# Retention mixer on one core: two turns for a chunk, first weights widened in pairs, projection tokens loaded ahead, key weights fetched in halves

## The chip, the cores and the metric

The kernel runs on one core of a Trainium2 chip. The metric is the time of one execution in microseconds on the device. TensorE (PE) does the matrix products; VectorE (DVE), ScalarE (ACT) and GpSimd (POOL) convert, copy and add; SyncE (SP) does nothing but issue DMA transfers, one after the other.

## The reference

Three layers follow each other over 8 batches of 576 positions and 512 channels. The weights come as float64.

```python
# retention: 8 heads of 64
scores = scale * q @ k.T
Dmat   = where(rel >= 0, gamma[h] ** rel, 0)
x      = (scores * Dmat) @ v                    # (8, 576, 512)
# low-rank mix along the sequence (rank 32), then an MLP
h  = x.T @ U @ V
u  = x + h.T
x2 = u + relu(u @ w_ch1) @ w_ch2                # 512 -> 2048 -> 512
# channel mix with the row before
xk = mu_k * x2 + (1 - mu_k) * x2_prev
xr = mu_r * x2 + (1 - mu_r) * x2_prev
k  = relu(xk @ w_k)                             # 512 -> 1024
out = sigmoid(xr @ w_r) * (k * k @ w_v)         # 1024 -> 512
```

## The kernel before

All products run as three passes over float32 numbers cut in a high and a low part (`split`: ScalarE casts the high part, `h`; another engine subtracts it, `l`): high by high weight, high by low weight, low by high weight. The float64 weights are brought in as pairs of words and turned into float32 by `widen` (L132 to L146: one ACT and four DVE instructions), then split.

Attention goes over 40 chunks, five to a batch (four of 128 rows and one of 64). `chunk_step` writes a chunk's TensorE work: `ds` (state), `xn` (transpose), `x` (values), `g` (the low-rank sum of the chunk before) and `s` (scores of the chunk after). VectorE masks the scores into `pm`, on which `x` depends. When a batch is through, `gt` is summed and eight mixes `mx` follow, whose results VectorE adds to `xt`; then `xt` is stored as `u` to DRAM (`ub`), in blocks of 512 rows that the nine blocks t of the MLP use. `hidden_tokens(t)` loads a block of u back, casts it (`uh`) and subtracts (`u` then holds the low part).

`hidden` gives, for each of the nine blocks, 16 tiles of 12 matmuls (`h_g_q`), which are fed into the attention, one at a time. `w1`, the first weight, is converted in eight units of 128x1024; a unit's low part is `w1l`. Tiles with an even q need units 0 to 3, tiles with an odd q units 4 to 7. ReLU results `h_o` go to DRAM (`hb`).

The projection (`Project`) has nine blocks of eight steps; a step takes one loaded piece of h (`y_x`), builds sums of blocks (`y_t`, mostly POOL), splits it (`y_kh` on ACT, low part on DVE) and does 42 matmuls for seven products. At a block's end `sums` combines eight PSUM banks on DVE into `y_s`, POOL adds u (`uin`) and the block x2 is stored (`xb`). Keys, gate and values follow, block by block: `load_x2` brings a block of x2 in (`x2in`), `mix_row` makes `m_x` and `zx` on ACT and DVE.

Three things set the order. TensorE's instructions stand in the order in which the code writes them. On the other engines a scheduler orders them by priority: the conversion of weights (`background`) stands behind the rest. SP issues the DMAs in its own order, and one that must wait holds all behind it. Weights of later phases go to DRAM and come back through `fetches`, when `limit` lets them, and all big tiles share one pool of 20 buffers (`RAWS`).

```python
for _ in chunk_step(i) ...:      # four turns to a chunk
    mixes(2 if i < JOIN else 1)
    pump(1 if i < 4 else 3 if i < JOIN else 2)
    drive(1)
```

`mixes(n)` writes so many mixes, `pump(n)` so many steps of weight conversion, `drive(n)` so many steps of the token loads in `ahead`. From chunk JOIN on, 16/5 hidden tiles go with each chunk.

## Time and profile before

| | |
|---|---|
| median of two runs | 1569.79 us (1569.6 to 1569.98) |
| profiled execution | 1573.2 us |
| its span | 1571.4 us |
| PE busy | 1469.6 us (94%) |
| DVE, ACT, POOL busy | 863.1, 561.8, 542.0 us |
| mean granted TensorE clock | 0.966 |

TensorE is busy nearly all the time, so a reader looks for the few places where it is not. In the page's slices it falls below full in the first three (up to 118 us), at 629 to 668 us, and from about 1021 us on. The granted clock is lowest in the same slices.

### The profile page before, as it was taken

The page shows a single profiled execution, that of the slowest core. Times are in us where ns is not written, and L with a number is a line of the kernel's source. Part 1 is how long each engine was busy: PE and PEld are TensorE (multiplying, and loading weights), DVE is VectorE, ACT ScalarE, POOL GpSimd, SP SyncE. Part 2 cuts the span into 40 slices and gives each one's busy share as a digit, 9 for nine tenths or more (in the row PEclk, how much of TensorE's full clock was granted, in tenths as well). Part 3 has the DMA queues.
Part 4 walks back from the last instruction along what each step waited for, and adds up shares of the span by engine and source line. Part 5 has one row for each costly group of instructions (what it writes and reads, how often), then busy time and mean ns, then how long its engine had stood idle before and what let it go on. Part 6 is the DMA issues. An engine that isn't in the chain of part 4 may idle for free. (4 is left out here: it accounts for less than half of the span.)

```text
span 1571.4 us, 24443 instructions
## 1 busy us (share of the span) xinstructions
PE 1469.6 (94%) x10164; PEld 1283.1 (82%) x10164; DVE 863.1 (55%) x1020; ACT 561.8 (36%) x822; POOL 542.0 (34%) x480
## 2 busy tenths in 40 slices
PE   7659999999999999699999999978999998999998
PEld 5547777777777888599999999978888888788887
DVE  4894554455631100278888888657676676443321
ACT  2533544444443222233333333244444445231210
POOL 3142433331210000267788778644334333000000
PEclk8869999999999999799999999989999999999999
DMA  9476897879834832724444444643323223875521
GB/s 322 169 266 215 310 331 287 311 268 344 321 146 165 343 134 105 290 96 147 159 150 162 161 158 151 227 189 133 135 111 131 108 111 131 329 281 206 205 103 54
DMA packets 76302, 312.97 MB, mean 199 GB/s; under 512 B 10080, under 2 KB 18528, under 8 KB 58272
## 3 DMA queue, kind: packets, MB, share of 16 engines
q1 hardware_dynamic: 76192, 311.42, 54.2%
q8 instruction: 80, 1.31, 0.3%
q14 instruction: 30, 0.25, 0.0%
HBM read 188.70 MB, written 122.68 MB: 198 GB/s over the span
## 5 line engine op out<-in xcount | busy, mean ns | idle before, releaser
L303 POOL TENSOR_TENSOR y_t<-y_x 128x256 f32<-128x256 f32 x72 | 81.6, 1133 | 256.1 <-DMA y_x<-hb 246.7
L412 PE MATMUL h<-uh,w1h 128*128 128x512 f32 x576 | 162.5, 404 | 1.8 <-ACT xt L575 1.8
L303 POOL TENSOR_TENSOR y_t<-y_x,y_t 128x256 f32<-128x256 f32 x144 | 160.1, 1112 | 11.3
L436 ACT ACTIVATE h_o<-h 128x512 f32<-128x512 f32 x144 | 84.7, 598 | 220.0 <-PE h L412 219.8
L412 PE MATMUL h<-uh,w1l 128*128 128x512 f32 x576 | 156.1, 393 | 0.9 <-DVE w1l L155 0.9
L412 PE MATMUL h<-u,w1h 128*128 128x512 f32 x576 | 155.2, 391 | 0.0
L412 PEld LDWEIGHTS h<-uh,w1l 128*128 128x128 f32 x576 | 108.9, 189 | 25.5 <-DVE w1l L155 1.3
L412 PEld LDWEIGHTS h<-u,w1h 128*128 128x128 f32 x576 | 108.7, 189 | 23.6
L490 POOL TENSOR_TENSOR qkv<-qkv,qtab 128x512 f32<-128x512 f32 (+1 forms) x35 | 46.7, 1333 | 225.0 <-DMA qkv<-in_qkv 169.5
L412 PEld LDWEIGHTS h<-uh,w1h 128*128 128x128 f32 x576 | 102.7, 189 | 24.3 <-issue 3.7
L303 DVE TENSOR_TENSOR y_t<-y_x 128x256 f32<-128x256 f32 x72 | 62.0, 861 | 89.1 <-DMA y_x<-hb 88.8
L303 POOL TENSOR_TENSOR m_x<-m_x 128x256 f32<-128x256 f32 x72 | 84.6, 1193 | 72.6 <-DVE m_x L900 54.5
L982 DVE TENSOR_TENSOR rin<-v,rin 128x512 f32<-128x512 f32 x36 | 24.8, 690 | 114.4 <-PE v L412 114.3
L516 DVE TENSOR_TENSOR pm<-s,mask 128x512 f32<-128x512 f32 (+1 forms) x80 | 47.6, 629 | 67.4 <-PE s L507 67.4
L412 PE MATMUL v<-vh,wvh 128*128 128x512 f32 x288 | 73.1, 395 | 3.4 <-ACT vh L153 3.4
L153 ACT CAST vh<-v 128x1024 fp32r<-128x1024 f32 x36 | 36.1, 1051 | 105.2 <-PE v L412 63.1
L412 PE MATMUL v<-vh,wvl 128*128 128x512 f32 x288 | 72.7, 396 | 0.0
L412 PE MATMUL v<-v,wvh 128*128 128x512 f32 x288 | 71.2, 389 | 0.0
L360 POOL TENSOR_TENSOR k_o<-k_o 128x512 f32<-128x512 f32 x18 | 23.8, 1324 | 127.0 <-issue 39.1
L412 PEld LDWEIGHTS v<-vh,wvh 128*128 128x128 f32 x288 | 54.2, 190 | 16.4 <-ACT vh L153 5.4
L878 POOL TENSOR_TENSOR uin<-uin,y_s 128x512 f32<-128x512 f32 x36 | 55.5, 1564 | 31.3 <-DVE y_s L377 31.2
L412 PEld LDWEIGHTS v<-vh,wvl 128*128 128x128 f32 x288 | 55.2, 192 | 11.7
(293 smaller groups left out, 4160.3 us busy)
## 6 DMA issues: line engine op xcount, KB each, us to landing
hb<-h_o SPq DMA_DIRECT2D x36, 1024.0 KB, 5.0
y_x<-hb SPq DMA_DIRECT2D x72, 512.0 KB, 4.7
qkv<-in_qkv SPq DMA_DIRECT2D x64, 512.0 KB, 7.5
kb<-k_o SPq DMA_DIRECT2D x18, 1024.0 KB, 3.9
v<-kb SPq DMA_DIRECT2D x18, 1024.0 KB, 6.9
u<-ub SPq DMA_DIRECT2D x9, 1024.0 KB, 9.8
uin<-ub SPq DMA_DIRECT2D x9, 1024.0 KB, 5.0
xb<-uin SPq DMA_DIRECT2D x9, 1024.0 KB, 4.8
```

Source lines behind the costliest of these rows:

```text
L153: nc.scalar.copy(h, x)
L303: engines[n % len(engines)].tensor_tensor(o, i, j, op=ALU.subtract)
L360: nc.gpsimd.tensor_tensor(c[1][1], c[1][1], c[1][0], op=ALU.add)
L412: nc.tensor.matmul(ps, weight.part(lo, k, o), x, start=(i == 0), stop=(i == len(todo) - 1))
L436: nc.scalar.activation(tile_of(outs[g], q), ps, AF.Relu)
L490: eng.tensor_tensor(q, q, qtab[:, c, :, :n], op=ALU.mult)
L516: nc.vector.tensor_tensor(p[:n, g, :, :n], ps[g][:n, :, :n], mask[:n, :, :n].to_broadcast([n, NP, n]), op=ALU.mult,)
L878: nc.gpsimd.tensor_tensor(v[:, i, :, j], v[:, i, :, j], c[i][j], op=ALU.add)
L982: nc.vector.tensor_tensor(r[:, o], ps, r[:, o], op=ALU.mult)
```

## The change

The chunk step yields twice instead of four times; the numbers per turn are doubled. `g` of the chunk before now stands ahead of `s` of the chunk after. Hidden tiles may begin with chunk 7 instead of 11, and before each tile the code makes sure that the four units of w1 that it needs are converted; block 0 takes the eight tiles with even q first, as the last block does. While w1 is converted, two units are pumped in turn, and the low part of w1 is subtracted by GpSimd, not VectorE.

In the projection, `begin` (loads and splits of the first pieces) is written inside the last hidden block, ten tiles from the end, instead of behind the last tile. At a block's end the splits of the next block's second piece and of its third stand in other places: `cut(s + 2)` runs at k = 7 ahead of `sums`, and `uin` is loaded at k = 4 instead of 0. The weights `wk[1]` and `wr` are asked for behind the projection's loop, not ahead of it.

```diff
--- before.py
+++ after.py
@@ -36,7 +36,7 @@
 RAWS = 20
 MORE = 5
-JOIN = 11
+JOIN = 7
 RATE = 16 / 5
@@ -92,20 +92,27 @@
     begun = set()
     ahead = []
+
+    width = [1]
+    turn = [0]
+
+    def step(x):
+        begun.add(id(x))
+        with tc.high_priority(offset=-LOW):
+            next(x)
+
     def pump(n):
         while n and background:
-            for x in background[1:2]:
+            for x in background[width[0]:width[0] + 1]:
                 if id(x) not in begun:
-                    begun.add(id(x))
-                    with tc.high_priority(offset=-LOW):
-                        next(x)
-            begun.add(id(background[0]))
+                    step(x)
+            turn[0] += 1
+            x = background[turn[0] % min(width[0], len(background))]
             try:
-                with tc.high_priority(offset=-LOW):
-                    next(background[0])
+                step(x)
                 n -= 1
             except StopIteration:
-                background.pop(0)
+                background.remove(x)
     def drive(n=None):
         while ahead and (n is None or n > 0):
@@ -149,10 +156,10 @@
         )
         yield
-    def split(h, l, x):
+    def split(h, l, x, eng=nc.vector):
         nc.scalar.copy(h, x)
         yield
-        nc.vector.tensor_tensor(l, x, h.bitcast(F32), op=ALU.subtract)
+        eng.tensor_tensor(l, x, h.bitcast(F32), op=ALU.subtract)
         yield
     def slot(x, i):
@@ -211,7 +218,7 @@
             self.per = 1024 // self.cols or 1
             self.units = self.rows * self.cols // 1024
-            self.parts = None
+            self.parts, self.finished = None, 0
         def keep(self):
             self.parts = [[raw(F32R, f"{self.nm}{lo}{i}") for i in range(self.units // 2)] for lo in "hl"]
@@ -244,7 +251,8 @@
             f, a = x[:, 1024:], x[:, :1024]
             yield from widen(f, a, w)
             if direct:
-                yield from split(self.unit(0, u), self.unit(1, u), f)
+                yield from split(self.unit(0, u), self.unit(1, u), f, nc.gpsimd)
+                self.finished += 1
                 return
             yield from split(a.bitcast(F32R), f.bitcast(F32R), f)
             for lo, y in enumerate((a, f)):
@@ -393,6 +401,7 @@
     tokens = {}
     stored = set()
+    done_tiles = [0]
     def hidden_tokens(t):
         x = raw(F32, f"u{t}")
@@ -424,13 +433,15 @@
             now = [(tile_of(h, k), tile_of(l, k), k) for k in range(KD)]
             asked = False
             tiles = [(g, q) for g in range(4) for q in range(4)]
-            if t == NB - 1:
+            if t in (0, NB - 1):
                 tiles.sort(key=lambda x: x[1] % 2)
             outs, missing = {}, {}
             for g, q in tiles:
                 if g not in outs:
                     outs[g], missing[g] = raw(F32, f"h{t}_{g}_o"), 4
+                while w1.finished < (q % 2 + 1) * w1.rows:
+                    pump(1)
                 ps = bank(f"h{t}_{g}_{q}")
                 plain(ps, q % 2 * 8 + g * 2 + q // 2, w1, now)
                 nc.scalar.activation(tile_of(outs[g], q), ps, AF.Relu)
@@ -651,7 +662,7 @@
         def later(b):
-            todo.extend([lambda: None] * 3)
+            todo.extend([lambda: None] * 2)
             for s in range(2):
                 for k in range(KD):
                     todo.append(lambda k=k, s=s: mix(b, k, s))
@@ -747,11 +758,7 @@
                 state(b, c)
             if i > 0:
                 natural(*seq[i - 1])
-            yield
             values(b, c, qs.pop(i))
-            yield
-            if i + 1 <= LAST:
-                scores(*seq[i + 1])
             yield
             if i > 0:
                 pb, pc = seq[i - 1]
@@ -759,6 +766,8 @@
                 if pc == NC - 1:
                     low_rank_sum(pb)
                     later(pb)
+            if i + 1 <= LAST:
+                scores(*seq[i + 1])
             yield
         def end_step():
@@ -778,33 +787,35 @@
         def later_weights():
             if not asked:
                 asked.append(1)
-                pump(1000)
+                width[0] = 1
                 background.extend(w.prepare() for w in (*w2, *wk[0], *wk[1]))
                 background.extend(wr.prepare(u, False) for u in range(wr.units))
                 background.extend(wv.prepare(u, False) for u in range(wv.units))
         def advance():
-            more = next(along, None)
-            return more is False
+            more = next(along, None) is False
+            done_tiles[0] += more
+            return more
         started = False
         for i in range(LAST + 2):
             if i == W_START:
                 w1.keep()
                 background.extend(w1.prepare(u, True) for u in range(w1.units))
+                width[0] = 2
             for _ in chunk_step(i) if i <= LAST else end_step():
-                mixes(2 if i < JOIN else 1)
+                mixes(4 if i < JOIN else 2)
                 if not started and 0 in stored:
                     ahead.append(hidden_tokens(0))
                     started = True
-                pump(1 if i < 4 else 3 if i < JOIN else 2)
-                drive(1)
+                pump(2 if i < 4 else 6 if w1.finished < w1.units else 4)
+                drive(2)
                 if i < JOIN:
                     continue
-                if i == JOIN:
+                if w1.finished == w1.units:
                     later_weights()
-                due += RATE / 4
+                due += RATE / 2
                 while due >= 1:
                     due -= 1
                     if not advance():
@@ -854,10 +865,12 @@
         def run(self):
             for s, (t, k) in enumerate(self.steps):
                 self.load(s + 2)
-                self.cut(s + 1)
+                if k or not t:
+                    self.cut(s + 1)
                 self.blocks(s + 2)
                 if k == 0:
                     acc = {p: bank(f"y{t}_{i}") for i, p in enumerate(ORDER)}
+                if k == 4:
                     u_in[t] = raw(F32, f"uin{t}")
                     nc.sync.dma_start(u_in[t].rearrange("p (k n) -> p k n", k=KD), u_blk[t])
                 assert w2[k].ready, k
@@ -868,6 +881,7 @@
                 if t == NB - 1:
                     w2[k].free()
                 if k == 7:
+                    self.cut(s + 2)
                     self.finish(t, sums(acc, f"y{t}"))
         def finish(self, t, c):
@@ -991,23 +1005,23 @@
         project = Project()
         for n, x in enumerate(along):
             if len(background) == 0:
-                limit[0] = 10
+                limit[0] = 10 if n < 16 * NB - 8 - done_tiles[0] else 14
             between(2, 1)
+            if n == 16 * NB - 10 - done_tiles[0]:
+                ahead.append(project.begin())
             if x:
                 drive()
         pump(1000)
         drive()
         limit[0] = 16
         supply()
-        ahead.append(project.begin())
         drive()
-        fetches.extend((*wk[0], *wk[1], wr))
+        fetches.extend(wk[0])
         for n, (t, k) in enumerate(project.run()):
             if n == 56 * NB - 24:
                 ahead.append(key_tokens(0))
-            if t == NB - 1:
-                limit[0] = 16 if n < 56 * NB - 20 else 12
             between(0, 1)
+        fetches.extend((*wk[1], wr))
         limit[0] = 10
         drive()
         supply()
@@ -1024,7 +1038,7 @@
             if t == NB - 1:
                 ahead.append(value_tokens(0))
             for _ in gate(t):
-                between(0, 3)
+                between(0, 4)
             if t == NB - 1:
                 wr.free()
             drive()
```

On TensorE at the start of the second hidden block, the kernel before (`mx` belongs to batch 1; `h_3_3` is the last tile of the first block and `h_0_0` the first of the second; `uh` and `u` its parts):

```order
L583 MATMUL xn_2_1246<-ident,xt_957 128x128 x4
L630 MATMUL mx_3_1_1253<-vst,gt_977 128x320
L412 MATMUL h_1_2_1258<-uh_776,w1h_371 128x512 x2
...
L412 MATMUL h_3_3_1567<-u_757,w1h_374 128x512 x2
L533 MATMUL ds_1454<-qkv_1_1231 64x64 x8
L583 MATMUL xn_0_1597<-ident,xt_1498 128x128 x4
L555 MATMUL x_1_1606<-qkv_1_1231,wst_193 128x128 x4
L565 MATMUL x_1_1606<-pm_1_1516,qkv_1_1231 64x128 x8
L412 MATMUL h_0_0_1623<-uh_1328,w1h_371 128x512 x2
```

Ten tiles stand between the last mix of batch 1 and the first tile of the second block. The changed kernel there:

```order
L641 MATMUL mx_2_1_1379<-vst,gt_1108 128x320
L641 MATMUL mx_3_1_1382<-vst,gt_1108 128x320
L544 MATMUL ds_1046<-qkv_3_1041 64x64 x8
L594 MATMUL xn_2_1404<-ident,xt_1073 128x128 x4
L566 MATMUL x_3_1411<-qkv_3_1041,wst_193 128x128 x4
L576 MATMUL x_3_1411<-pm_3_1366,qkv_3_1041 64x128 x8
L614 MATMUL g_1223<-xs_2_1409,ust 32x128 x4
L518 MATMUL s_4_0_1447<-qkv_4_1162 64x64
...
L594 MATMUL xn_3_1470<-ident,xt_1073 128x128 x4
L566 MATMUL x_4_1477<-qkv_4_1162,wst_192 128x64 x4
L576 MATMUL x_4_1477<-pm_4_1446,qkv_4_1162 64x64 x8
L421 MATMUL h_0_0_1497<-uh_1440,w1h_371 128x512 x2
```

No tile is left between the two; one chunk's work and half of another's stand there.

On SP at the end of the hidden phase, the kernel before (`hb_3_110` is the store of the last tiles, `w_7h` and `w_7l` the last projection weight, `y_k_x` the loads of the pieces):

```order
L197 DMA w_7h<-w_7_d_161 128x1792
L439 DMA hb_2_109<-h_2_o 128x2048
L198 DMA w_7l<-w_7_d_162 128x1792
L439 DMA hb_3_110<-h_3_o 128x2048
L833 DMA y_0_x<-hb_0_75 128x1024
L833 DMA y_1_x<-hb_0_75 128x1024
L833 DMA y_2_x<-hb_1_76 128x1024
```

The changed kernel, from the end of the last block but one to the end of the last:

```order
L450 DMA hb_3_106<-h_3_o 128x2048
L844 DMA y_0_x<-hb_0_75 128x1024
L844 DMA y_1_x<-hb_0_75 128x1024
L204 DMA w_5h<-w_5_d_157 128x1792
...
L450 DMA hb_3_110<-h_3_o 128x2048
L204 DMA w_7h<-w_7_d_161 128x1792
L205 DMA w_7l<-w_7_d_162 128x1792
L844 DMA y_2_x<-hb_1_76 128x1024
```

The loads of pieces 0 and 1 now stand ahead of the last hidden block's stores, and that of piece 2 behind the last weight's.

On SP in the last projection block, the kernel before (`wk` key weights, `wrh` and `wrl` the gate's, `x2in` the blocks of x2 for the keys, `xb_119` the store of the last one):

```order
L833 DMA y_6_x<-hb_3_110 128x1024
L197 DMA wk_11h<-wk_d_169 128x1792
L198 DMA wk_11l<-wk_d_170 128x1792
L888 DMA x2in_9119<-xb_111 128x2048
L833 DMA y_7_x<-hb_3_110 128x1024
L263 DMA wrh_9159<-wr_d_171 128x2048
L263 DMA wrl_9160<-wr_d_172 128x2048
L881 DMA xb_119<-uin_8855 128x2048
L888 DMA x2in_9448<-xb_112 128x2048
```

The changed kernel there:

```order
L902 DMA x2in_9111<-xb_111 128x2048
L844 DMA y_7_x<-hb_3_110 128x1024
L205 DMA wk_10l<-wk_d_168 128x1792
L204 DMA wk_11h<-wk_d_169 128x1792
L205 DMA wk_11l<-wk_d_170 128x1792
L895 DMA xb_119<-uin_9079 128x2048
L271 DMA wrh_9325<-wr_d_171 128x2048
L271 DMA wrl_9326<-wr_d_172 128x2048
L902 DMA x2in_9448<-xb_112 128x2048
```

The first `x2in` stands ahead of three key-weight loads, and the second behind the gate's weights, whose loads now stand behind `xb_119`.

## Rows read from the trace of the kernel before

**Rows 1.** Busy us (instructions) of PE, PEld, DVE, ACT, POOL; granted clock, DMA share, GB/s.

```profile
44.00:110.00 66.00, 36.71 (x362) 29.11 (x359) 60.58 (x62) 30.85 (x51) 20.58 (x12) 0.68 0.59 217
652.00:668.00 16.00, 8.28 (x35) 7.69 (x36) 8.62 (x8) 5.44 (x6) 10.72 (x12) 0.50 0.61 231
720.00:760.00 40.00, 38.75 (x323) 38.55 (x323) 32.95 (x31) 14.04 (x16) 31.30 (x28) 1.00 0.43 140
997.00:1056.00 59.00, 45.71 (x336) 43.78 (x335) 33.00 (x42) 18.37 (x23) 31.22 (x31) 0.91 0.66 259
```

**Rows 2.** Waits of TensorE, 40 to 125 us: total, times, longest.

```profile
PE x L565 <- DVE pm L516: 14.2, 6, 10.2
PE s L507 <- POOL qkv L490: 8.3, 2, 6.9
PE mx L630 <- DVE gt L621: 6.0, 1, 6.0
```

**Rows 3.** Timeline of TensorE: start, length, operation [idle before it].

```profile
109.78 1.91 PE L412 MATMUL h<-uh,w1h 128*128 128x512 f32 x4
```

**Rows 4.** Timeline of the DMA queue on SyncE, first block of u.

```profile
66.93 0.58 SPq L642 DMA_DIRECT2D ub<-xt  x1
...
72.14 1.04 SPq L399 DMA_DIRECT2D u<-ub  x1
```

**Rows 5.** Timeline of VectorE, conversions of w1 units.

```profile
87.46 1.22 DVE L155 TENSOR_TENSOR w1l<-w_x,w1h 128x1024 fp32r<-128x1024 f32 x1
...
90.81 2.06 DVE L134 SCALAR_TENSOR_TENSOR w_x<-w_x,w_raw 128x1024 f32<-128x1024 f32 x1
```

**Rows 6.** Timeline of GpSimd, the scaling of v.

```profile
10.36 1.04 POOL L495 TENSOR_TENSOR qkv<-qkv,vtab 128x512 f32<-128x512 f32 x1 [8.64 <-DMA qkv<-in_qkv]
...
89.77 2.02 POOL L495 TENSOR_TENSOR qkv<-qkv,vtab 128x512 f32<-128x512 f32 x1
```

**Rows 7.** Groups of TensorE's instructions, 120 to 360 us: count, busy, mean ns.

```profile
L412 PE MATMUL h<-uh,w1h 128*128 128x512 f32 x223 | 64.3, 410 | 1.8 <-ACT xt L575 1.8
...
L507 PE MATMUL s<-qkv 64*128 64x128 f32 (+1 forms) x272 | 17.8, 270 | 0.0
```

**Rows 8.** Timeline of VectorE, last mix addition of batch 1.

```profile
139.96 0.48 DVE L634 TENSOR_TENSOR xt<-mx,xt 128x320 f32<-128x320 f32 x1
```

**Rows 9.** Timeline of ScalarE, casts of the second block of u.

```profile
157.79 1.05 ACT L153 CAST uh<-u 128x1024 fp32r<-128x1024 f32 x1 [3.39 <-DMA u<-ub]
...
159.71 1.05 ACT L153 CAST uh<-u 128x1024 fp32r<-128x1024 f32 x1
```

**Rows 10.** Timeline of ScalarE, end of the hidden phase.

```profile
644.81 0.60 ACT L436 ACTIVATE h_o<-h 128x512 f32<-128x512 f32 x1 [2.12 <-PE h L412]
647.53 0.60 ACT L436 ACTIVATE h_o<-h 128x512 f32<-128x512 f32 x1 [2.12 <-PE h L412]
655.36 0.83 ACT L153 CAST y_0h<-y_x 128x768 fp32r<-128x768 f32 x1 [7.23 <-DMA y_x<-hb]
```

**Rows 11.** Waits of TensorE, 640 to 700 us.

```profile
PE y L328 <- ACT y_0h L153: 8.7, 1, 8.7
PE y L328 <- DVE y_x L155: 3.5, 2, 2.6
```

**Rows 12.** Timeline of GpSimd at one boundary of two projection blocks.

```profile
749.44 3.97 POOL L878 TENSOR_TENSOR uin<-uin,y_s 128x512 f32<-128x512 f32 x3
```

**Rows 13.** Timeline of ScalarE at the same boundary.

```profile
753.44 1.05 ACT L153 CAST y_2h<-y_t 128x1024 fp32r<-128x1024 f32 x1 [9.30 <-POOL uin L878]
```

**Rows 14.** Timeline of ScalarE, mixing rows of x2 for the keys.

```profile
1034.82 1.33 ACT L894 ACTIVATE m_x<-x2in,omu 128x511 f32<-128x511 f32 x2 [8.08 <-DMA x2in<-xb]
...
1073.35 0.72 ACT L894 ACTIVATE m_x<-x2in,omu 128x511 f32<-128x511 f32 x1 [4.70 <-DMA x2in<-xb]
```

**Rows 15.** Waits of TensorE, 1000 to 1090 us.

```profile
PE y L328 <- ACT y_6h L153: 4.6, 1, 4.6
PE k_x L328 <- ACT k_o L345: 2.1, 1, 2.1
```

## The prediction

> **What bounds the kernel now.** The page comes first: TensorE is busy 1469.6 of 1571.4 us, so the kernel is as long as its matmuls plus the stretches in which TensorE waits or runs at the lower granted clock. Nothing in the change takes matmuls away. The slices show where such stretches lie, the stretch table what each costs, and the waits and timelines what ended last in each.
>
> There are four. **Start:** between 44 and 110 us TensorE is busy 36.7 of 66 us at a mean clock of 0.68 [rows 1], so 29.3 us are idle, and 36.7 x 0.32 = 11.7 us go to the clock. It waits for masked scores behind VectorE (14.2 us), for scaled q and k (8.3) and for the low-rank sum (6.0) [rows 2]; VectorE is busy 60.6 of the 66 us [rows 1], and conversions of w1 are most of that. The first hidden tile starts at 109.78 [rows 3]. **From hidden to projection:** the last ReLU is at 647.53 [rows 10], then waits of 8.7 and 3.5 us [rows 11], and 8.3 us of work at 0.50 [rows 1], 4.1 us lost: some 16.5 with the small rest. **Block boundaries:** 38.75 busy of 40 us in a stretch that holds one boundary [rows 1], 1.25 us at each of eight, 10 us. **Last projection block and first keys:** 45.7 busy of 59 us at 0.91 [rows 1], 13.3 idle and 4.1 for the clock; one wait is 4.6 us, and the first key step waits 2.1 [rows 15]. In the rest of the hidden phase and from the second key block on, TensorE has nothing left to wait for that the change touches: from 1075 us on the instructions stand in the same order on every engine.
>
> **A, the start.** With g ahead of s, the sum for the mixes is ready some 5.5 us sooner, and by following each engine's new order with the durations of the old rows I get: mixes from about 45 us, last addition 61.4, store of u 61.5. In the trace before, u is loaded 5.2 us after its store [rows 4], where SP has other loads between; the store has to land first, so I keep 5.2: issued at 66.7, landed about 72, first cast done 73.3. Hidden tiles begin there, 36.5 us sooner than at 109.78. TensorE then idles about 9 us ahead of that tile, and the attention work that the kernel before had done by 109.78 and this one has not is about 16 us, plus some 2 at the lower clock: 36.5 - 16 - 2 = 18.5 us in hand.
>
> The second half of w1, which odd tiles need, I put at 97 to 105 us, where its first tile comes at about 110: no wait, with little cover. The price if that cover goes is a microsecond for each that it is late.
>
> Most of the gain is lost again at the second hidden block. Its u is complete only with batch 1. Before, ten tiles stand between that batch's last mix and the first tile of the block, 2.72 us each from the spacing of the last two ReLUs [rows 10]; now none does, because tiles began earlier and the mixes' rate was kept. What stands there is a chunk and a half. A chunk costs about 4.4 us: between 120 and 360 us 223 high matmuls make 56 tiles or 152 us, and the other 86 us are 17 chunks (272 score matmuls, 16 to a chunk) [rows 7] with 0.7 of mixes in each. So the cover is some 7 us. The way through DRAM took, from the last addition, 139.96 + 0.48 [rows 8], to the end of the second cast, 159.71 + 1.05 [rows 9], 20.3 us. A first tile can begin a little before the second cast ends, so 17 to 19 us against 7: 10 to 12 us of wait, and 2 to 3 us for the clock after it, since rows show 0.50 after the wait of 8.7 us [rows 1, 11]. That takes 14 of the 18.5: **A = +4 us**. Ends: +16 if the wait does not come (loads of u have a shorter queue before them), -5 if the chain takes 28 us. From the third block on 23 to 30 us of cover stand there against the same 17 to 22, and I cost them at nothing.
>
> The move of the low subtraction to GpSimd is the place to doubt. Rows show that the two engines disturb each other: a VectorE operation of 128x1024 takes 1.22 us while GpSimd idles and 2.06 while it scales q and v [rows 5]; GpSimd's 128x512 takes 1.04 us alone and 2.02 beside VectorE [rows 6]. The moved operation is twice that size, so 2.1 to 4 us each, eight times; VectorE is relieved of 8 x 1.22 = 9.8 us and may lose as much again while GpSimd runs. I take that as a wash, between -7 and +10 us of VectorE time. The Trainium skill (SBUF — State Buffer, "Who interferes with whom") says that a VectorE instruction with two SBUF inputs and a GpSimd instruction that reads SBUF exclude each other for a whole instruction. By that rule the eight subtractions block VectorE 8 x 2.1 = 16.6 us to save 9.8, and VectorE ends 7 us later, not sooner; the rows agree in kind.
>
> **B, hidden to projection.** The loads of pieces 0 and 1 now stand ahead of the last hidden block's stores, and their casts between its tiles, so steps 0 and 1 run behind the last tile at once: two steps of 5.04 us (38.75 us for 323 matmuls [rows 1], 42 to a step), to 657.6. Piece 2 is new as the late one: its load stands on SP behind the last store of h and both parts of the last weight, which wait for the buffers of the last tile. That is 1.0 + 1.8 + 0.5 MB from 648.2 on; at 392 GB/s (259 at a DMA share of 0.66 [rows 1]) 8.7 us, so it lands at about 657. Piece 0 needed 0.9 us from its first cast to a first product and, with its sums of blocks, some 6 to the last, by the start of its cast [rows 10] and the waits behind it [rows 11]. I take 4 to 6 us of wait and 3 for the clock: **B = 16.5 - 8 = +8.5**. Ends: +14 if piece 2 is hardly late, +3 if it costs as much as piece 0 did.
>
> **C, eight boundaries.** Before, the cast of piece 2 waits 9.30 us for GpSimd's additions of u [rows 13], which run until 753.41 [rows 12], because it reuses the buffer of the sums. Now the splits of piece 1 come ahead of the sums and that of piece 2 waits for the step before alone. But VectorE's sums start about 1 us later for it, GpSimd's additions about 2, and piece 3's blocks on GpSimd (busy 31.3 of 40 us [rows 1]) end later: its low part would be there at about 762.5, against a need at 761.1. I take half of the gain, **C = +5**, between 0 and +10.
>
> **D, last block.** ScalarE waits 8.08 us for the first x2 block and holds the cast of piece 6 behind itself [rows 14, 15]. Three key-weight loads (2.75 MB) now stand behind that load and one of u (1.05 MB) ahead: 1.7 MB less, 4.3 us at 392 GB/s. That helps two steps and the clock after them, about +8. In return the gate's weights (2.1 MB), loaded early before, now stand ahead of the second x2 block, which comes 5.4 us later; the first key step waited 2.1 us for it, behind ScalarE [rows 14, 15], and would wait some 7: -5. **D = +3**, between -5 and +10.
>
> Turns in place of quarter turns leave the rates as they were, and the other limits on fetches move loads that nobody waits for; nothing for these.
>
> **The rivals.** (1) *The gains stay.* The second block's u comes without a wait and pieces 2 and 3 are in time: 16 + 14 + 10 + 3 = 43 us, 1527. For it: DMA is quieter early on. Against: the cover of 7 us. (2) *The waits only move.* Piece 2 costs what piece 0 did, piece 3 takes over at the boundaries and the second x2 block eats D: 4 + 3 + 0 - 5 = 2 us, about 1568. For it: each of the three is named above with a queue in front. (3) *The port.* GpSimd's subtractions slow VectorE so that the second half of w1 is late by 5 to 10 us: 1555 to 1560. For it: VectorE's 60.6 of 66 us. Against: the distance to the need. The rule of the Trainium skill given under A (SBUF — State Buffer, "Who interferes with whom") would have it so. (4) *Slower: every hidden block waits for its u.* SP issues in order, and if stores of h and of converted weights that wait for TensorE stand ahead of each load of u, the trip grows beyond the cover in all of the blocks of the attention. The gain is gone at 20.5 / 7, about 3 us in each of seven; with 35 us against 29.5 it is 5.5 x 7 = 38 us, 1588. Against: the trip in the rows took 20.3 us [rows 8, 9].
>
> **How the numbers follow.** 4 + 8.5 + 5 + 3 = 20.5 us off the profiled execution of 1573.2 is 1552.7; that execution lies 3.4 us above the median of 1569.79, so on the median's footing 1549.3, told as 1550. Chances: the forecast (1540 to 1560) 0.50; (1) 0.16; (2) 0.18; (3) 0.09; (4) 0.07. The range of 8 in 10 is 1531 to 1571: below it lies half of (1), above it (4) and a little of (2). Two per cent, which is about what a measurement here tells from no change, are 1538.4 and 1601.2: faster by more 0.17, within 0.79, slower by more 0.04 (the far part of (4)).
>
> **What would show it.** In the profile after: a first hidden tile near 73 us; one wait of about 10 us of a hidden tile for a cast of u between 150 and 170 us; no wait right after the last hidden tile, but one of a few microseconds two steps later; windows at boundaries above 39 of 40 us; the first key step waiting longer than 2.1 us. The forecast falls if any wait of the hidden blocks repeats from block to block, or if the start takes VectorE as long as before.

## The result and the profile after

The changed kernel takes 1586.83 us (median of two runs, 1586.27 to 1587.39) against 1569.79: a ratio of 1.0109, 95% interval 1.0065 to 1.0152. It is slower, where 1550 was forecast. Its profiled execution spans 1584.5 us, 13.1 more than before; the stages below are of these two executions.

The stretch table of the changed kernel (busy us of PE, PEld, DVE, ACT, POOL, then granted clock, DMA share, GB/s); the first, third, fourth and fifth rows answer to [rows 1]:

```profile
44.00:110.00 66.00, 47.53 (x342) 37.15 (x343) 61.26 (x54) 28.63 (x43) 42.34 (x19) 0.77 0.51 182
159.00:177.00 18.00, 7.06 (x36) 4.80 (x36) 9.62 (x7) 5.02 (x5) 6.87 (x6) 0.53 0.88 347
671.00:680.00 9.00, 7.75 (x42) 7.46 (x43) 8.38 (x8) 4.17 (x5) 7.47 (x7) 0.61 0.01 3
760.00:800.00 40.00, 38.21 (x315) 37.60 (x314) 31.16 (x31) 13.06 (x15) 29.50 (x28) 1.00 0.37 140
1006.00:1062.00 56.00, 47.12 (x339) 45.80 (x339) 32.05 (x41) 19.39 (x24) 31.64 (x31) 0.88 0.61 235
```

Between 44 and 110 us TensorE is busy 11 us more than before. VectorE is as full as it was (61.3 of 66, 60.6 before), though the subtractions of w1 have left it, and GpSimd is busy twice as long (42.3 against 20.6); "if the start takes VectorE as long as before" was one of the prediction's own signs against it. Then comes a hole: 7 of 18 us busy at a clock of 0.53, in a stretch in which the kernel before had no idle time. A second stretch matters below, 200 to 400 us. Both in the kernel before:

```profile
159.00:177.00 18.00, 18.00 (x141) 13.53 (x139) 11.84 (x11) 11.47 (x21) 9.14 (x8) 1.00 0.84 335
200.00:400.00 200.00, 198.20 (x1490) 155.08 (x1489) 101.63 (x115) 88.47 (x144) 59.24 (x61) 0.99 0.86 309
```

The waits of TensorE in the changed kernel (total, times, longest), 40 to 125 us, 120 to 600, 600 to 700 and 1050 to 1120, in this order:

```profile
PE h L421 <- ACT uh L160: 7.7, 1, 7.7
PE mx L641 <- DVE gt L632: 6.2, 1, 6.2
PE x L576 <- DVE pm L527: 3.1, 3, 2.6
PE mx L641 <- ACT vst L699: 3.0, 1, 3.0
...
PE h L421 <- ACT uh L160: 12.5, 1, 12.5
PE g L614 <- ACT xs L604: 4.1, 2, 3.3
PE x L576 <- DVE pm L527: 2.0, 2, 1.3
...
PE y L336 <- ACT y_2h L160: 4.7, 1, 4.7
PE y L336 <- DVE y_x L162: 3.5, 2, 2.6
...
PE k_x L336 <- ACT k_o L353: 8.0, 1, 8.0
```

The masked scores cost 3.1 us instead of 14.2 [rows 2], but the mixes wait as long for their sum as before. The second hidden block waits 12.5 us for its u; g waits for its transposed rows, which it never did. The wait behind the last hidden tile (8.7 and 3.5 us [rows 11]) has become one of 4.7 and 3.5 for piece 2, and the first key step waits 8.0 instead of 2.1 [rows 15].

One boundary in the changed kernel, the timelines of GpSimd, ScalarE and SyncE (block start 788.24):

```profile
789.08 1.30 POOL L892 TENSOR_TENSOR uin<-uin,y_s 128x512 f32<-128x512 f32 x1 [4.69 <-DVE y_s L385]
...
795.98 2.27 POOL L892 TENSOR_TENSOR uin<-uin,y_s 128x512 f32<-128x512 f32 x1
...
805.51 0.83 ACT L160 CAST y_4h<-y_x 128x768 fp32r<-128x768 f32 x1 [2.94 <-issue]
...
798.28 0.32 SPq L895 DMA_DIRECT2D xb<-uin  x1
798.65 2.46 SPq L844 DMA_DIRECT2D y_x<-hb  x3
```

The cast of piece 4 in the kernel before, in the block that starts at 745.99:

```profile
760.19 0.84 ACT L153 CAST y_4h<-y_x 128x768 fp32r<-128x768 f32 x1 [0.30 <-DMA y_x<-hb]
```

GpSimd's additions now end 10.0 us after the block's start (798.25), where they ended 7.4 after it before [rows 12]; x2's store, and the load of piece 4 behind it, follow at once. The cast of piece 4 begins 17.3 us after the block's start instead of 14.2. The wait has moved from step 2 to step 4. Over the seven blocks from the second to the last but one, TensorE's waits grow only from 8.8 us (seven of them) to 11.7 (thirteen). Some 5 us more are busy time for the same matmuls (289.0 against 284.2 us), at a granted clock of 0.99 instead of 1.00: behind two of the waits it is 0.50 for 3 us.

In the code only one split moves, that of a block's second piece (from k = 0 to k = 7 of the block before); the third piece is split at k = 1 as before. So the loop has two edits, this split and the later load of u.

By the first and last matmul of each stage, before and after: to the last hidden matmul 647.5 and 653.3 us; on to the second projection block 56.7 and 51.8; seven blocks 292.8 and 301.1; the last block 59.3 and 55.9; keys and gate up to the last of the gate 307.6 and 314.9; the values 207.5 both. So +5.8, -4.9, +8.3, -3.4, +7.3: 13.1 us.

### The profile page after: what moved, and what is told of

Its sections match the earlier page's. It is cut to its first block, busy times and chain, and to the rows that moved or that the text cites. A ratio compares the mean times of both kernels' runs of the same rounds, so it can differ in the third digit from the quotient of the medians.

```text
span 1584.5 us, 24463 instructions
## 1 busy us (share of the span) xinstructions
PE 1474.5 (93%) x10164; PEld 1289.6 (81%) x10164; DVE 848.5 (54%) x1012; ACT 562.1 (35%) x822; POOL 544.6 (34%) x488
## 5 line engine op out<-in xcount | busy, mean ns | idle before, releaser
L311 POOL TENSOR_TENSOR y_t<-y_x 128x256 f32<-128x256 f32 x72 | 73.3, 1017 | 263.0 <-DMA y_x<-hb 244.4
L421 PEld LDWEIGHTS h<-uh,w1h 128*128 128x128 f32 x576 | 106.0, 193 | 44.9 <-ACT uh L160 21.4
L311 POOL TENSOR_TENSOR y_t<-y_x,y_t 128x256 f32<-128x256 f32 x144 | 137.7, 956 | 10.7
L501 POOL TENSOR_TENSOR qkv<-qkv,qtab 128x512 f32<-128x512 f32 (+1 forms) x35 | 49.4, 1411 | 195.7 <-DMA qkv<-in_qkv 129.9
L311 DVE TENSOR_TENSOR y_t<-y_x 128x256 f32<-128x256 f32 x72 | 62.2, 872 | 59.3 <-DMA y_x<-hb 59.3
L506 POOL TENSOR_TENSOR qkv<-qkv,vtab 128x512 f32<-128x512 f32 (+1 forms) x40 | 57.3, 1433 | 31.2 <-DMA qkv<-in_qkv 30.0
```

Source lines behind the costliest of these rows:

```text
L311: engines[n % len(engines)].tensor_tensor(o, i, j, op=ALU.subtract)
L421: nc.tensor.matmul(ps, weight.part(lo, k, o), x, start=(i == 0), stop=(i == len(todo) - 1))
L501: eng.tensor_tensor(q, q, qtab[:, c, :, :n], op=ALU.mult)
L506: nc.gpsimd.tensor_tensor(v, v, vtab[:n, c].to_broadcast([n, H, D]), op=ALU.mult)
```

## The experiments

All ratios are to the kernel before, timed on the same chip.

**1. The old block loop** (a_noR).

```diff
-                if k or not t:
-                    self.cut(s + 1)
+                self.cut(s + 1)
-                if k == 4:
-                    u_in[t] = ...; load of u
+                if k == 0: (in the block that makes acc) load of u
                 if k == 7:
-                    self.cut(s + 2)
                     self.finish(t, sums(acc, f"y{t}"))
```

> The changed kernel with the projection's block loop as it was before (the splits of pieces 1 and 2 and the load of u back in their old places). Theory: that loop costs 8.3 us over the seven block lengths between the second and the last block (301.1 against 292.8 in the two profiles), so this kernel takes 1586.8 - 8 = about 1578 us, with one wait of 1.25 us a third into step 2 of every block and none at step 4. Rival: the blocks are longer because of what comes ahead of them (pieces loaded early, the other starting positions of the buffers), and the loop is innocent: 1586 to 1588, and waits of 1.6 us at step 4 stay.

Measured: 1.0023 (1.0004 to 1.0042). The seven blocks take 292.9 us, with 1.25 us at step 2. The loop costs 8 us in them, and the last block is 3 us shorter as well (53.0): 11 us by the stages, some 13 by the ratios.

**2. The store of x2 behind the load of piece 4** (a_xbLate).

```diff
                 self.load(s + 2)
+                if k == 2 and t:
+                    nc.sync.dma_start(*self.late)      # the store of block t - 1
...
-            nc.sync.dma_start(x2_blk[t], whole)
+            self.late = x2_blk[t], whole               # the last block's at once
```

> The changed kernel, but the store of a finished block of x2 is issued behind the load of piece 4 of the next block instead of ahead of it (the last block's at once). Theory: the waits of 1.6 us at step 4 come from that load standing on SP behind a store that waits for GpSimd's additions; without it they go, all boundaries are free of waits, and the time falls by the 12 us idle and 3 us of clock that the profile shows in the seven blocks, to 1572 to 1576. Rival: the two engines that do the sums of blocks are late by themselves, GpSimd above all; then a wait of over 1 us stays at step 3 or 4 and the time falls by under 4 us.

Measured: 1.0085 (1.0065 to 1.0105); the waits at step 4 go, but others of 1.7 to 2.75 us come at step 3 in five of the seven blocks, which take 299.0 us. The theory as put fails. The load of piece 4 is issued at 797.2 in the block that starts at 787.2, no sooner than before: it got the buffer of the sums, which the same additions free. And VectorE now has piece 4 ahead of piece 3's low part, as its timeline shows:

```profile
801.85 0.42 DVE L311 TENSOR_TENSOR y_t<-y_x 128x256 f32<-128x256 f32 x1 [4.31 <-DMA y_x<-hb]
802.19 1.76 DVE L162 TENSOR_TENSOR y_x<-y_t,y_3h 128x1024 fp32r<-128x1024 f32 x1
```

**3. Four mixes to a turn** (a_mix4).

```diff
-                mixes(4 if i < JOIN else 2)
+                mixes(4)
```

> The changed kernel with four mixes to a turn all the way, so that the mixes of batch 1 are written one chunk earlier and four tiles of the first hidden block stand behind them. Theory: the wait of 12.45 us at 169.94 is the way of u through DRAM (17 us from the last addition to the end of its cast) less a cover of 7; with some 17 us of cover it falls to under 3 us, the clock after it stays, and the time falls by 10 to 15 us, to 1572 to 1577. Rival: the wait only moves, because the mixes now wait for VectorE or the batch's last sums, or the next blocks lose what this one wins: within 3 us of 1587.

Measured: 1.0129 (1.0096 to 1.0162), not faster. The waits of TensorE from 120 to 600 us:

```profile
PE mx L641 <- DVE gt L632: 15.0, 7, 3.2
PE h L421 <- ACT uh L160: 4.1, 1, 4.1
```

The wait for u fell from 12.5 to 4.1 us, as the cover theory has it; but the first mixes now come in the turn of their own sum and wait for it in each of seven batches, 15 us. Both theories saw a part.

**4. All late weights asked for early** (a_noK).

```diff
-        fetches.extend(wk[0])
+        fetches.extend((*wk[0], *wk[1], wr))        # and the limits of before
...
-        fetches.extend((*wk[1], wr))
```

> The changed kernel with all key weights and the gate's weights asked for ahead of the projection's loop, as before, and the old limits. Theory: asking late helps the last block (3.4 us shorter in the profile) and costs 7.3 us behind it, where the second block of x2 stands behind the gate's weights and the first key step waits 8.0 us instead of 2.1; so undoing it gives 4 us back: 1582 to 1584, with the key step's wait at about 2. Rival: the wait of the key step comes from x2 being stored later, not from the weights ahead of its load: the wait stays over 5 us and the time at 1587 or above.

Measured: 1.0085 (1.0057 to 1.0114), which the intervals don't separate from the changed kernel. The key step's wait falls from 8.0 to 1.9 us, but one of 6.5 for piece 6 takes its place, as before [rows 15]; the last block takes 61.7 us (55.9), the stage behind it 310.2 (314.9). The wait went as the theory has it, but the two stages sum to 1 us more, not 4 less: give and take, at about even.

**5. Mixes four to a turn and a turn later** (n_mixB), on the kernel of experiment 1.

```diff
-                mixes(4 if i < JOIN else 2)
+                mixes(4)
-            todo.extend([lambda: None] * 2)
+            todo.extend([lambda: None] * 4)
```

> The changed kernel with the old block loop (the kernel of the first experiment, 1.0023 of before, some 1573 us), and the mixes of a batch four to a turn, begun a turn later. Theory: the wait of 11.6 us ahead of the second hidden block is short cover for the way of u through DRAM; five tiles and two chunks' work now stand there, about 22 us against 17, and the batch's sum has a turn to be ready in, so the waits of mixes for it (1.6 to 3.2 us a batch with four to a turn from the first) do not come: 10 to 15 us less, 1558 to 1563, and no wait over 1 us of a hidden tile from 120 to 600 us. Rival: the mixes wait for their sums again, 1.6 to 3 us in each batch, and the time stays at 1570 or above.

Measured: 0.9938 (0.9916 to 0.9960), from 1.0023. The wait for u is 3.1 us, no mix waits for its sum after the first batch, and the last hidden matmul ends 6.8 us sooner.

**6. Scores ahead of the low-rank products** (n_gs), on the kernel of experiment 1.

```diff
             yield
+            if i + 1 <= LAST:
+                scores(*seq[i + 1])
             if i > 0:
                 ... low_rank(pb, pc), low_rank_sum, later
-            if i + 1 <= LAST:
-                scores(*seq[i + 1])
             yield
```

> The same kernel of the first experiment, with the scores of the next chunk written ahead of the low-rank products of the one before, as in the kernel before. Theory: the waits of g for its transposed rows (3.3 and 1.4 us) and of x for the masked scores (0.7 and 1.35), with the clock after them, come from that order, which leaves less work between a step and its user; they go and the time falls by 5 to 9 us to 1564 to 1568, though the first mixes wait some 1 us longer. Rival: these waits are ScalarE's, behind casts of weights that wait for GpSimd, and come in either order: within 3 us of 1573.

Measured: 0.9945 (0.9920 to 0.9971), more than expected: the hidden phase ends at 637.2 instead of 650.3 us. The mixes wait 10.5 us for their sum instead of 6.2 and the first tile still comes 3.5 us sooner; the waits of g and x from 250 to 360 us are gone, and so are 14 of the 55 us of the hidden phase that ran at the lower clock.

**7. The gate's weights behind the second block of x2** (n_wr), on the kernel of experiment 1.

```diff
-        fetches.extend((*wk[1], wr))
+        fetches.extend(wk[1])
             for _ in keys(t):
                 between(0, 2)
+                if t == 0 and 1 in x2_in and not wr.ready:
+                    fetches.append(wr)
+                    supply()
```

> The same kernel of the first experiment, with the gate's weights asked for behind the load of the second block of x2 and the store of the first keys. Theory: the first key step waits 7.2 us for ScalarE, which waits for that load, which stands behind 2.1 MB of gate weights; with the weights behind it the wait falls to about 2 and the time by 4 to 6 us, to 1567 to 1569. Rival: the load comes late because the store of the last block of x2 ahead of it waits for GpSimd; then the wait stays over 5 us. If the weights come too late now, the gate waits for them instead, and the time rises.

Measured: 0.9974 (0.9959 to 0.9989). The wait falls from 7.2 to 4.2 us and the stage from 314.2 to 310.2. The gate's weights are the larger part of the wait's growth, not all.

**8. The last projection weight behind pieces 2 and 3** (n_w7), on the kernel of experiment 1.

```diff
-        limit[0] = 16
-        supply()
         drive()
...
+            if n == 7:
+                limit[0] = 16
             between(0, 1)
```

> The same kernel of the first experiment, with the last projection weight asked for behind the loads of pieces 2 and 3. Theory: piece 2 comes late (waits of 7.8 and 1.1 us) because its load stands behind 1.8 MB of that weight; without it, it lands 4.7 us sooner, the waits fall to 3 to 5 and the time by 5 to 7 us with the clock, to 1566 to 1568. Rival: its load is held by something else, the buffer that it goes to or the last store of h, and the waits stay above 7 us, or the last weight is late at step 7.

Measured: 1.0007 (0.9991 to 1.0024). The waits for piece 2 fall from 7.8 and 1.1 to 4.2 and 1.1, the stretch up to the second block from 51.4 to 47.9 us. So the weight is part of what holds piece 2, and over half of the wait stays without it. Of the 5 to 7 us expected the ratios show some 2.5, which the intervals do not separate from nothing.

**9. Experiments 1, 5, 6, 7 and 8 together** (best).

> The changed kernel with the old block loop and all four corrections at once: scores ahead of the low-rank products, mixes four to a turn and a turn later, the last projection weight behind pieces 2 and 3, the gate's weights behind the second block of x2. Theory (the four act in different stretches): from the profiles, the start and hidden phase 637 less some 6 for the second hidden block's wait, the way into the projection 48, seven blocks 293, the last 53, the keys 310: about 1545 us, a ratio of 0.983. Rival: the two corrections of the start are not additive, since both shorten the same wait, and the ratio is 0.989 or above.

Measured: 0.9890 (0.9870 to 0.9910): the rival's number, though not its reason. The projection's parts add up (49.0, 293.1, 52.0, 306.7), but the hidden phase ends at 644.5, later than with experiment 6 alone: the first tile at 80.65, and a second wait of 7.7 us for the low part of u, while no wait for u from 120 to 600 us is over 3.4 us.

**10. The same with VectorE's subtraction** (best_dve).

```diff
-                yield from split(self.unit(0, u), self.unit(1, u), f, nc.gpsimd)
+                yield from split(self.unit(0, u), self.unit(1, u), f)
```

> The kernel with all corrections, but the low part of w1 subtracted by VectorE as before. Theory of the port (and of the prediction's doubt): the subtraction on GpSimd disturbs VectorE as much as it relieves it, so the time is within 3 us of the kernel with all corrections. Rival A: the move helps; VectorE has 9.8 us more to do in the start, the first tile comes 3 to 6 us later, and the time rises by 3 us or more. Rival B: the exclusion costs more than it saves; the time falls by 3 us or more.

Measured: 0.9829 (0.9805 to 0.9853), rival B: 10.7 us of hidden phase (633.8). The groups of both kernels from 30 to 110 us (count, busy, mean ns), first with GpSimd's subtraction, then with VectorE's:

```profile
L141 DVE SCALAR_TENSOR_TENSOR w_x<-w_x,w_raw 128x1024 f32<-128x1024 f32 x8 | 13.9, 1741 | 2.1 <-ACT w_x L139 2.1
L153 DVE SCALAR_TENSOR_TENSOR w_x<-w_raw,w_x 128x1024 uint32<-128x1024 uint32 x8 | 12.5, 1560 | 0.2
L162 POOL TENSOR_TENSOR w1l<-w_x,w1h 128x1024 fp32r<-128x1024 f32 x8 | 21.2, 2661 | 31.0 <-ACT w1h L160 25.2 <-issue 5.8
```

```profile
L162 DVE TENSOR_TENSOR w1l<-w_x,w1h 128x1024 fp32r<-128x1024 f32 x8 | 11.8, 1493 | 0.0
L141 DVE SCALAR_TENSOR_TENSOR w_x<-w_x,w_raw 128x1024 f32<-128x1024 f32 x8 | 10.8, 1348 | 0.6 <-ACT w_x L139 0.6
L153 DVE SCALAR_TENSOR_TENSOR w_x<-w_raw,w_x 128x1024 uint32<-128x1024 uint32 x8 | 9.7, 1220 | 0.1
```

GpSimd needs 21.2 us for what VectorE does in 11.8, and two groups of VectorE alone get 5.9 us longer meanwhile. Half of the relief is lost, and each unit's low part takes 2.7 us instead of 1.5.

**11 and 12. Half of the loop undone: u loaded at the first step again** (a_uin0); **the splits back in their places** (a_cutOld).

```diff
-                if k == 4:
+                if k == 0:                       # a_uin0
                     u_in[t] = ...; load of u
```

```diff
-                if k or not t:                   # a_cutOld
-                    self.cut(s + 1)
+                self.cut(s + 1)
                 if k == 7:
-                    self.cut(s + 2)
```

> The changed kernel with u loaded at a block's first step again, and the new places of the splits kept. Theory: the splits of pieces 1 and 2 ahead of the sums make the block longer, because VectorE begins the sums 2.6 us later, GpSimd's additions of u end later by as much, and the load of piece 4 has to wait for them; so the seven blocks stay at 299 to 302 us and the time at 1584 to 1588. Rival: it is the load of u in the middle of a block that is in the way of the pieces; then the seven blocks fall to 292 to 295 and the time by 7 us or more.

> The changed kernel with the splits in their old places and u still loaded at the block's fifth step. Theory: all of the 8 us of the loop come from the splits, so the seven blocks take 292 to 294 us with 1.25 us at step 2 of each, and the time is 1573 to 1578 like the kernel with the whole loop undone. Rival: the late load of u holds a part, and the blocks take 296 us or more.

Measured: a_uin0 1.0220 (1.0195 to 1.0245), seven blocks 322.2 us; a_cutOld 1.0074 (1.0054 to 1.0094), 298.1 us with 1.56 at step 4. Neither theory nor rival: the two edits don't add, the new splits need the late load (322 against 301) and the late load alone loses 5 (298 against 293). In a_uin0 it is piece 3 that stands behind x2's store on SyncE; it lands 14 us after the block's start and is needed a microsecond later (timelines of SyncE and ScalarE, block start 796.3):

```profile
802.15 0.32 SPq L894 DMA_DIRECT2D xb<-uin  x1
802.59 9.38 SPq L844 DMA_DIRECT2D y_x<-hb  x5
...
810.39 0.83 ACT L160 CAST y_3h<-y_x 128x768 fp32r<-128x768 f32 x1 [6.45 <-DMA y_x<-hb]
```

The two also tell the edits' effects apart. The first cast of piece 2 (ScalarE), in a_uin0 and then in a_cutOld (block start 785.3):

```profile
802.16 1.05 ACT L160 CAST y_2h<-y_t 128x1024 fp32r<-128x1024 f32 x1 [9.31 <-POOL uin L891]
```

```profile
785.47 0.84 ACT L160 CAST y_2h<-y_x 128x768 fp32r<-128x768 f32 x1 [2.05 <-PE y L336]
```

With the new place of the split alone, piece 2 still waits 9.3 us for GpSimd's additions, as in the kernel before [rows 13]; with the later load of u alone it waits for TensorE's step, as in the changed kernel. And with the split alone VectorE's sums begin 3.3 us before the block's start, as in the kernel before (0.7 in the changed kernel), and the additions end 5.8 us after it, sooner than the 7.4 of before: the split by itself does not make them late.

**13. GpSimd issues the store of x2** (a_xbPool).

```diff
-            nc.sync.dma_start(x2_blk[t], whole)
+            nc.gpsimd.dma_start(x2_blk[t], whole)
```

> The changed kernel, but GpSimd issues the store of x2 itself, behind its own additions, so that SP's loads stand behind it no more and keep their buffers. Theory: the load of piece 4 is then held by VectorE's sums alone, is issued some 6 us sooner, and the wait at step 4 goes; the seven blocks take 292 us or less (301.1 before this) and the time falls by 8 to 14 us, to 1573 to 1579. Rival: VectorE and GpSimd are late with their own work on pieces 3 and 4, or GpSimd loses time to the issue; then waits of over 1 us a block stay and the blocks take 297 us or more.

Measured: 1.0122 (1.0102 to 1.0142), seven blocks 310.0 us. The buffers did not stay: piece 4 again got one that GpSimd's additions free, and GpSimd now waits for its load ahead of piece 3's blocks. This says nothing clear of SyncE's order, and the rival's bound (297) is passed.

**14 and 15. One part undone on the changed kernel itself:** the subtraction (a_dve, the diff of 10) and the order of scores (a_gs, the diff of 6).

> The changed kernel with the low part of w1 subtracted by VectorE again, nothing else. Theory: on GpSimd each takes some 2.6 us, in which VectorE's operations with two inputs stand still, so VectorE gains nothing and the chain of a unit gets longer; the time falls by 6 to 10 us, to 1577 to 1581. Rival: that loss belongs to the corrected kernels, where VectorE alone sets the start; here other waits cover it, and the time stays within 3 us of 1587.

> The changed kernel with the scores of the next chunk written ahead of the low-rank products again, nothing else. Theory: as with the old block loop, the hidden phase gets 11 to 15 us shorter, half of it at the lower clock: 1572 to 1576, and no wait for transposed rows or masked scores over 1 us from 200 to 400 us. Rival: part of that gain was the other start of that run: under 8 us.

Measured: a_dve 1.0061 (1.0039 to 1.0082), some 7.5 us less by the ratios, whose interval overlaps that of the changed kernel; its profile shows only 2.3 us of it in the hidden phase (651.0). a_gs 1.0024 (1.0010 to 1.0037), 13 us less, clear of noise; by the profile 9.7 us of it lie in the hidden phase (643.5). The stretch from 200 to 400 us of the changed kernel and of a_gs:

```profile
200.00:400.00 200.00, 193.90 (x1466) 154.05 (x1465) 100.78 (x108) 82.76 (x133) 63.19 (x60) 0.97 0.79 290
```

```profile
200.00:400.00 200.00, 198.52 (x1528) 158.14 (x1527) 106.53 (x116) 89.65 (x146) 66.56 (x62) 0.99 0.83 301
```

Some 5 us of idle time and the lower clock after it are the order's, in a stretch for which the prediction named no wait; a_gs is back at the idle time of the kernel before (198.20 us busy).

**16. The changed loop, with GpSimd's store, on the best kernel** (best_xp; the loop of the change and the diff of 13).

> The best kernel so far (all corrections, VectorE's subtraction, 0.983) with the changed block loop and GpSimd issuing the store of x2. If a_xbPool's theory holds, the 1.25 us at each boundary go and the seven blocks take 284 to 288 us instead of 293: 1537 to 1542 us, a ratio of 0.978 to 0.981. If not, 0.983 or above.

Measured: 0.9990 (0.9973 to 1.0008), seven blocks 310.5 us: the loop with this store costs 17 us there, and the blocks are as long as in experiment 13.

**17. Units of w1 one at a time, on the best kernel** (best_w1).

```diff
-                width[0] = 2
+                width[0] = 1
```

> The best kernel (0.983), with the units of w1 widened one at a time as before, the number of steps to a turn unchanged. Theory: two at a time put conversions of w1 between those of V, and the mixes wait 2.3 us for V's low part; one at a time V is ready first, that wait goes, the units' chains are no later in sum, and the first hidden block waits no longer: within 3 us of 1546, or up to 4 us less. Rival: one unit alone leaves VectorE idle between its dependent steps with ScalarE, the last of the four units comes later and the first tile with it; the time rises by 3 us or more, with a wait for w1's low part at the first tiles.

Measured: 0.9886 (0.9863 to 0.9910), the rival's side: on this kernel widening in pairs is worth 9 us. The mixes no longer wait for V, but the first tiles wait 16.9 us for u (5.8 in best_dve, both parts), as the waits of TensorE from 40 to 125 us show:

```profile
PE h L421 <- ACT uh L160: 16.9, 2, 12.4
PE mx L641 <- DVE xt L645: 2.5, 2, 2.0
```

The rival named a wait for w1; it is the casts of u that come late, because on ScalarE they stand behind casts of w1 that wait for VectorE:

```profile
73.32 1.04 ACT L160 CAST w1h<-w_x 128x1024 fp32r<-128x1024 f32 x1 [6.37 <-DVE w_x L153]
...
75.31 1.04 ACT L160 CAST uh<-u 128x1024 fp32r<-128x1024 f32 x1
80.04 1.04 ACT L160 CAST w1h<-w_x 128x1024 fp32r<-128x1024 f32 x1 [3.69 <-DVE w_x L153]
80.99 1.04 ACT L160 CAST uh<-u 128x1024 fp32r<-128x1024 f32 x1
```

## Why the prediction was wrong

**A, the start: +4 forecast, -5.8 measured.** The picture was right in its milestones: the first tile at 75.2 us (73.3 said), one wait of 12.5 us of the second hidden block (10 to 12 said), and after it a stretch at a clock of 0.53. Experiments 3 and 5 show the cause as told: with more tiles or work between, the wait falls to 4.1 and 3.1 us. Busy time times granted clock tells what each stretch is worth. The hole from 159 to 177 us takes 14.3 us (7.06 x 0.53 against 18.0 x 1.00), where 14 was forecast. But the start gives some 12 us up to 110 us (47.53 x 0.77 against 36.71 x 0.68), where 18.5 was forecast, and 200 to 400 us, put at nothing, takes some 8 (193.90 x 0.97 against 198.20 x 0.99).

Three steps failed. The first is "In the rest of the hidden phase and from the second key block on, TensorE has nothing left to wait for that the change touches". The second belongs to it: "With g ahead of s, the sum for the mixes is ready some 5.5 us sooner" counted a gain and no cost. The first mix does come sooner by it (49.1 us against 54.6 in experiment 15, 49.4 against 50.9 in 6), though it waits 6.2 us for its sum as before; but the order costs 10 to 13 us of the hidden phase (experiments 15 and 6), since g now follows closer on the rows that ScalarE copies for it, and x on the scores that VectorE masks. Their waits go when the order is undone.

The third is "I take that as a wash" for the subtraction. On the kernel with the corrections, half of the 11.8 us that leave VectorE come back as longer operations, each subtraction takes 1.2 us longer, and the eighth low part of w1 ends at 110.1 us instead of 100.4 (experiments 9 and 10): 10 us in all. On the changed kernel it ends at 111.2 instead of 107.6 (experiment 14), and the 7 us of the ratios are not clear of noise. The rule of the Trainium skill (SBUF — State Buffer, "Who interferes with whom"), by which VectorE would end later and not sooner, had the direction right. VectorE's own busy time falls all the same, by 5.9 us in the groups of experiment 10. Widening in pairs, which I gave no price, gains 9 us on the best kernel (experiment 17). What the earlier tiles and the two turns are worth alone was not tested.

**B, hidden to projection: +8.5 forecast, +4.9 measured.** The mechanism was right: steps 0 and 1 run at once, and piece 2 is the late one. The term was mis-sized: waits of 8.1 us with 3 for the clock, not 4 to 6 and 3. Piece 2 came 13.8 us after the last hidden matmul (653.3), not 9.5 as reckoned (657 against 647.5):

```profile
667.11 0.83 ACT L160 CAST y_2h<-y_x 128x768 fp32r<-128x768 f32 x1 [11.53 <-DMA y_x<-hb]
```

The 3.3 MB counted ahead of it were not all that was under way: the store of h before the last, issued at 648.5, landed only at 656.7. Experiment 8 gives the weight's share of the wait, 3.6 of 8.9 us; how the rest is shared is not shown.

**C, boundaries: +5 forecast, -8.3 measured (in seven of the eight).** Two steps failed. One is the path: "its low part would be there at about 762.5, against a need at 761.1. I take half of the gain" follows piece 3 through GpSimd, but not the store of x2 and the load of piece 4 behind it, though the additions ahead of them were said to end about 2 us later. They end 2.6 us later, piece 4 is cast at 17.3 us after the block's start instead of 14.2, and the wait is at step 4. The other is a term that was put at nothing: the later load of u, which the prediction does not name. Alone it costs 5 of the 8 us (experiment 12), and it, not the split, is what frees piece 2 of its wait for the additions (experiments 11 and 12), which the prediction gave to the splits. Experiment 1 shows that the loop is the cause. That SyncE's order alone is the path is not shown: in experiments 2 and 13, which took the store away, buffers and the engines' order changed with it, and experiments 11 and 12 show that the two edits act on each other. Which of these holds a piece in each arrangement, only the traces tell, one by one.

**D, last block and keys: +3 forecast, -3.9 measured.** The key step's wait of 8.0 us was forecast (7), and 4.2 of experiment 7 shows the gate's weights as the larger part of its growth. The gain ahead of it was not 8 but 3.4 us. With the old loop (experiment 1) the gain is 6.3 us and the loss behind it 6.6, so the two stages take 367.2 us against 366.9 before: half of the 7 us that were missing are the loop's again, with a wait of 4.2 us for piece 4 (1.2 with the old loop), and the other half is a gain and a loss mis-sized by under 2 us each.

Of the rivals, (2) named two of the moves, piece 2 and the key step, and (3) the port; none had the three losses together, and (2) held them to be at worst a gain of 2 us. Rival (4) gives 1588, next to the measured 1586.83, but that is luck: its wait for u in each of seven blocks did not come, only the one of the second block.

## The version that beats both

The kernel of experiment 10, at 1546.55 us and a ratio of 0.9829 (0.9805 to 0.9853), is faster than both: the change's pairs, early tiles and early pieces, with the block loop, the order of scores and the subtraction of before, faster mixes, and two weights asked for later. Its waits of TensorE from 120 to 600 us:

```profile
PE h L421 <- ACT uh L160: 2.4, 2, 2.1
PE h L421 <- DVE pm L527: 1.6, 2, 1.4
PE s L518 <- ACT xt L586: 1.3, 1, 1.3
```

## What to carry to other kernels

An edit that moves a step closer to what it depends on has a price even if it helps what follows: cost both ends, and follow every load that stands behind the moved step's stores. Work begun earlier is kept only if what its next stage needs comes earlier by as much; here the mixes' rate decided that, not the start. A full engine is relieved by less than the operation that it hands over, if the two engines exclude each other while they run: here half of 11.8 us came back, and the operation itself took longer.

## What was unexpected of the hardware

GpSimd and VectorE hold each other up by whole instructions where both have two inputs. The timelines of VectorE and GpSimd in the kernel of experiment 9, first while GpSimd idles, then beside its subtraction:

```profile
69.30 1.22 DVE L153 SCALAR_TENSOR_TENSOR w_x<-w_raw,w_x 128x1024 uint32<-128x1024 uint32 x1
...
72.17 2.98 DVE L153 SCALAR_TENSOR_TENSOR w_x<-w_raw,w_x 128x1024 uint32<-128x1024 uint32 x1
...
91.00 2.35 DVE L162 TENSOR_TENSOR u<-u,uh 128x1024 fp32r<-128x1024 f32 x2
...
71.73 2.35 POOL L162 TENSOR_TENSOR w1l<-w_x,w1h 128x1024 fp32r<-128x1024 f32 x1 [5.82 <-issue]
...
92.23 3.34 POOL L162 TENSOR_TENSOR w1l<-w_x,w1h 128x1024 fp32r<-128x1024 f32 x1 [2.24 <-ACT w1h L160]
```

An operation that takes 1.22 us alone begins 0.44 us after GpSimd's and takes 2.98: GpSimd's ends at 74.08, 1.9 us on, and about its own 1.1 us follows. It goes the other way too: the subtraction that begins at 92.23, in VectorE's second of two on u, ends 2.2 us after VectorE has finished at 93.35, which is about its own length. That agrees with the rule named under A.
